# Moving the transposes of an attention and gated-layer kernel from TensorE to the DMA crossbar

## The chip, the cores and the metric

The kernel runs on one core of one Trainium2 chip. The metric is the time of one execution in microseconds of device time. Each run states how many executions it had, and gives their median with the lowest and highest. Every experiment ran beside the kernel before on the same chip.

## The reference, cut to what matters

Four batches of block-sparse attention (8 heads, 768 rows, head size 64; a window of 16 around each row, plus one maximum of k and one mean of v for each block of 32 rows) feed a gated layer of 512 inputs and 1536 hidden values. All inputs and the output are 32-bit floats in DRAM.

```python
k_sum = k.reshape(B, H, nb, 32, D).max(axis=3)
v_sum = v.reshape(B, H, nb, 32, D).mean(axis=3)
scores_l = where(|i - j| < 16, scale * q @ k.T, -1e9)
scores_s = scale * q @ k_sum.T + log(32)
a = softmax(concat([scores_l, scores_s]))
attn = a @ concat([v, v_sum])
x = attn.transpose(0, 2, 1, 3).reshape(B * S, H * D)      # 3072 x 512
out = (sigmoid(x @ w_gate) * (x @ w_val)) @ w_out
```

The kernel's matmuls sum along the partitions of their tiles. So q and k are turned, to have the head size on the partitions, and so are the normalised values, to have the 512 channels on them. These three transposes are what the change moves.

## The kernel before

While TensorE works on batch b's layers, the attention of batch b+1 is slipped in between as small units. A unit is a letter and a pair of heads: T transposes q and k of pair p and makes the block maxima, S makes scores and their exponentials, V the means of v, A multiplies with v and normalises, X transposes the result into xT, the input of the layers. The order of the units fixes the order of every engine's instructions.

```python
def load_qk(tap, b, p, half=None, queue=None):          # whole rows, uncast, SyncE
    (queue or nc.sync).dma_start(out=st..., in_=tap[b, 2*p:2*p+2, ...])

def T(self, p, h=None):
    self.transposed(pk, self.src[p][0])     # 6 x nc.tensor.transpose into PSUM
    self.transposed(pq, self.src[p][1])     # 6 more
    self.natural(kTn[:, 16:16 + S], pk)     # ScalarE copy out of PSUM
    self.natural(self.qT[p]..., pq)         # ScalarE copy out of PSUM
    nc.vector.tensor_reduce(...max...)      # then two VectorE copies into kTx
    ...
def X(self, p, h=None):
    ...                                     # 6 x nc.tensor.transpose of xs
    nc.scalar.copy(out=self.xT[:, p, o:o + n], in_=br[:, 0:n])

def replicate(self, t0):                    # spreads the means: vx <- vx, SyncE
    nc.sync.dma_start(out=vx[96:120, t0:NQ]..., in_=vx[96:120, 0:1]...to_broadcast(...))

def load_next(b):                           # q, k: load, then cast on GpSimd
    for p in range(NP):
        s_ = (load_qk(k, b, p), load_qk(q, b, p))
        srcs[b][p] = [cast_qk(s_[0], "pool"), cast_qk(s_[1], "pool")]

REST  = "Q0 Q1 S0b Q2 S1b Q3 S2b S3b A0b A1b X0b A2b X1b A3b X2b X3b"   # batch 0, half 2
FIRST = "T0 T1 S0a S0b T2 S1a S1b T3 S2a S2b V S3a S3b"                 # batch 1
LAST  = "- - A0 A1 X0 A2 X1 A3 X2 X3"
NEXT  = "- - T0 T1 S0a S0b T2 S1a S1b T3 S2a S2b S3a S3b - - A0 A1 X0 A2 X1 A3 X2 X3"
# [...] the layers of a batch, with the units spread among them
spread(m1[0] + m1[1] + ffn.units2(), extra, 0, 33)
```

v and all weights already come by casting loads from GpSimd (32-bit in DRAM, 16-bit in the on-chip memory). v's rows are 64 values of one head, so its pieces are 128 bytes as written.

The softmax here doesn't subtract the row's maximum and nothing guards it: scores larger than these inputs give would overflow.

Of the kernel before, what the change touches and what calls it, by code (L numbers as in the profile page):

```python
# [8 lines left out]
FP32 = mybir.dt.float32  # L9
BF16 = mybir.dt.bfloat16  # L10
# [6 lines left out]
def kernel(  # L17
# [10 lines left out]
    nc = tc.nc  # L28

    B, H, S, D = q.shape  # L30
# [4 lines left out]
    NS = S // 32  # L35
    KX = W + NS
    NP = H // 2
# [3 lines left out]
    HALF = S // 2  # L41

    const = ctx.enter_context(tc.tile_pool(name="const", bufs=1))
    stg_pool = ctx.enter_context(tc.tile_pool(name="stg", bufs=8))
    bf_pool = ctx.enter_context(tc.tile_pool(name="bf", bufs=10))
    vm_pool = ctx.enter_context(tc.tile_pool(name="vmp", bufs=2))
    qT_pool = ctx.enter_context(tc.tile_pool(name="qTp", bufs=4))
    p_pool = ctx.enter_context(tc.tile_pool(name="pp", bufs=4))
    xs_pool = ctx.enter_context(tc.tile_pool(name="xsp", bufs=2))
    xT_pool = ctx.enter_context(tc.tile_pool(name="xTp", bufs=2))  # L50
    hT_pool = ctx.enter_context(tc.tile_pool(name="hTp", bufs=2))
    gate_pool = ctx.enter_context(tc.tile_pool(name="gatep", bufs=3))
# [9 lines left out]
    def view(ap, off, dims):  # L62
        return bass.AP(ap.tensor, ap.offset + off, [list(ap.ap[0])] + [list(d) for d in dims])
# [5 lines left out]
    kTn_t = [const.tile([128, S + 32], BF16, name=f"kTn{i}") for i in range(2)]  # L69
# [51 lines left out]
        else:  # L121
            nc.gpsimd.tensor_copy(out=out, in_=in_)  # L122

    def load_qk(tap, b, p, half=None, queue=None):

        n = S if half is None else HALF
        s0 = 0 if half is None else HALF * half
        T = n // 128
        st = stg_pool.tile([128, 2, 6, 64], FP32, name="qkst", tag="stg")
        (queue or nc.sync).dma_start(  # L130
            out=st[:, :, 0:T, :].rearrange("p h t d -> p h (t d)"),
            in_=tap[b, 2 * p:2 * p + 2, s0:s0 + n, :].rearrange("h (p t) d -> p h (t d)", t=T),
        )
        return st[:, :, 0:T, :]

    def cast_qk(st, eng):
        T = st.shape[2]
        bf = bf_pool.tile([128, 6, 2, 64], BF16, name="qkbf", tag="qkbf")[:, 0:T]
        copy(eng, bf, st.rearrange("p h t d -> p t h d"))
        return bf  # L140

    def load_v(b, t0, t1):

# [23 lines left out]
    class Attention:  # L167
        def __init__(self, b, src, xT):


            self.b, self.src, self.xT = b, src, xT
            self.vx = vx_t[b % 2]
            self.kTx, self.qT, self.P, self.xs = {}, {}, {}, {}
            self.vm, self.ms = {}, {}

        def transposed(self, dst, src):
# [4 lines left out]
        def natural(self, dst, src):  # L181
# [2 lines left out]
            nc.scalar.copy(out=dst.rearrange("p (a t) -> p a t", t=T),  # L184
                           in_=src[:, 0:128 * T].rearrange("p (t a) -> p a t", t=T))

        def T(self, p, h=None):

            at = psum2.tile([128, 2, 1024], BF16, name="tp", tag="at")
            pk, pq = at[:, 0], at[:, 1]  # L190
            self.transposed(pk, self.src[p][0])
            self.transposed(pq, self.src[p][1])
            kTn, kTx = kTn_t[kT_ctr[0] % 2], kTx_t[kT_ctr[0] % 4]
            kT_ctr[0] += 1
            self.kTx[p] = kTx
            self.qT[p] = qT_pool.tile([128, S], BF16, name="qT", tag="qT")
            self.natural(kTn[:, 16:16 + S], pk)
            self.natural(self.qT[p][:, 0:S if h is None else HALF], pq)
            nc.vector.tensor_reduce(  # L199
                out=kTx[:, 0, W:KX],  # L200
                in_=kTn[:, 16:16 + S].rearrange("p (n w) -> p n w", w=32),
                axis=AX.X, op=ALU.max)
            nc.vector.tensor_copy(out=kTx[:, :, 0:W], in_=view(kTn, 0, [[QT, NQ], [1, W]]))  # L203
            nc.vector.tensor_copy(
                out=kTx[:, 1:NQ, W:KX],
                in_=kTx[:, 0:1, W:KX].to_broadcast([128, NQ - 1, NS]))

        def Q(self, p, h=None):

            pq = psum2.tile([128, 2, 1024], BF16, name="tp", tag="at")[:, 1]  # L210
            self.transposed(pq, self.src[p][2])
            self.natural(self.qT[p][:, HALF:S], pq)

        def S(self, p, hf):
            kTx, qT = self.kTx[p], self.qT[p]
# [42 lines left out]


        def L(self, g, h=None):  # L260
            st = self.vm[g] = vm_pool.tile([4 * NS, 32, 64], FP32, name="vm", tag="vm")
            nc.sync.dma_start(
                out=st.rearrange("p w d -> p (w d)"),
                in_=v[self.b, 4 * g:4 * g + 4].rearrange("h (n w) d -> (h n) (w d)", w=32))
            self.ms[g] = vm_pool.tile([4 * NS, 64], FP32, name="ms", tag="ms")
# [24 lines left out]
        def A(self, p, h=None):  # L290
# [6 lines left out]
            for t in range(6 * g0, 6 * g1):  # L297
# [14 lines left out]
                in1=rec[:, 0:G].to_broadcast([128, G, 6, 64]),  # L312
                op=ALU.mult)
            self.xs[p] = xs

        def X(self, p, h=None):
            n = S if h is None else HALF
# [62 lines left out]
    def spread(base, extra, lo, hi):  # L380

        n, m, j = len(base), len(extra), 0
        for i, u in enumerate(base):
            u()
            if i >= lo:
                want = min(m, (m * (i + 1 - lo) + (hi - lo) - 1) // (hi - lo))
                while j < want:
                    extra[j]()
                    j += 1
        while j < m:  # L390
            extra[j]()
            j += 1
# [6 lines left out]

    a0 = att[0]  # L400

    sk = [load_qk(k, 0, p) for p in range(NP)]
    sq = [load_qk(q, 0, p, half=0, queue=nc.scalar) for p in range(NP)]

    def cast0(p):
        srcs[0][p] = [cast_qk(sk[p], "dve"), cast_qk(sq[p], "act")]
# [28 lines left out]


    def load_next(b):
        for p in range(NP):
            s_ = (load_qk(k, b, p), load_qk(q, b, p))
            srcs[b][p] = [cast_qk(s_[0], "pool"), cast_qk(s_[1], "pool")]  # L440

    for p in range(NP):
        srcs[0][p].append(cast_qk(load_qk(q, 0, p, half=1), "pool"))
    for i in range(6):
        load_wo(i)
    load_next(1)
    load_v(1, 0, NQ)

    REST = "Q0 Q1 S0b Q2 S1b Q3 S2b S3b A0b A1b X0b A2b X1b A3b X2b X3b"
    FIRST = "T0 T1 S0a S0b T2 S1a S1b T3 S2a S2b V S3a S3b"  # L450
    LAST = "- - A0 A1 X0 A2 X1 A3 X2 X3"
    MEANS = "R0a R0b R0c R0d M0 R1a R1b R1c R1d M1 - B".split()
    NEXT = "- - T0 T1 S0a S0b T2 S1a S1b T3 S2a S2b S3a S3b - - A0 A1 X0 A2 X1 A3 X2 X3".split()

    def loads(b):
        if b < B:
# [5 lines left out]
    for b in range(B):  # L462
        ffn = f0 if b == 0 else Ffn(b, xTs[b])
        m1 = [[(lambda f=f, hf=hf: ffn.m1(f, hf)) for f in range(NF)] for hf in range(2)]
        if b == 0:
            spread(m1[0][1:], a0.units(REST), 2, 10)
            extra = att[1].units(FIRST) + [lambda: loads(2)] + att[1].units(LAST)
            spread(m1[1] + ffn.units2(), extra, 4, 23)
        else:
            extra = []  # L470
            if b + 1 < B:
                both = [x for pair in zip(MEANS, NEXT) for x in pair]
                extra = (att[b + 1].units(" ".join(both)) + [lambda: loads(b + 2)]
                         + att[b + 1].units(" ".join(NEXT[len(MEANS):])))
            spread(m1[0] + m1[1] + ffn.units2(), extra, 0, 33)


# [28 lines left out]
```

## Time and profile before

| | before |
|---|---|
| time, median of 3 (lowest to highest) | 261.75 us (260.33 to 263.04) |
| span of the profiled execution | 259.5 us |
| TensorE busy | 241.0 us |
| holes in TensorE after 28 us (sum of its timeline's idle times) | 2.3 us |
| first layer matmul of batch 0, 1, 2, 3 | 26.7, 95.2, 152.4, 208.7 us |

The last row is the ruler in this kernel. It cuts the span at the starts of the four batches.

The page cuts the span in 40 slices of 6.5 us. A digit is the busy share of a slice in tenths, PEclk the granted clock of TensorE, DMA the mean busy share of the 16 DMA engines:

```profile
PE   1567899999999998999999999999999999999993
...
PEclk9999999999999999999999999999999999999999
DMA  6999999999308999900199999000211220000132
```

TensorE is full from the sixth slice on and its clock is whole. From the twelfth slice on the DMA row has gaps: the transfers come in bursts with rest between.

### The profile page before, as it was taken

What the parts mean: (1) busy time and instruction counts of PE and PEld (TensorE: products, weight loads), DVE (VectorE), ACT (ScalarE), POOL (GpSimd) and SP (SyncE); (2) the same over time, 40 slices, a digit from 0 to 9 for tenths busy, and PEclk for the clock granted to TensorE, in tenths of its full rate; (3) what the DMA queues carried; (4) which work ended last, traced back from release to release, by engine and by line L of the source; (5) the groups of instructions that cost most, each with busy time, mean ns of one, the idle gap of its engine ahead of it and who ended that gap; (6) DMA issues with size and microseconds to landing.
All of it is one profiled execution on the core that took longest, in us unless ns stands there. A gap on an engine that the chain in (4) does not pass through costs nothing.

```text
span 259.5 us, 5305 instructions
## 1 busy us (share of the span) xinstructions
PE 241.0 (93%) x2136; PEld 137.7 (53%) x2136; DVE 133.8 (52%) x263; ACT 124.5 (48%) x217; POOL 77.1 (30%) x111
## 2 busy tenths in 40 slices
PE   1567899999999998999999999999999999999993
PEld 1432455666644555666555556666555556666441
DVE  5865237648733318888645227988543124444000
ACT  2850347538942434766742435766533433333111
POOL 8998059377000279400002893000000000000000
PEclk9999999999999999999999999999999999999999
DMA  6999999999308999900199999000211220000132
GB/s 223 230 165 170 222 269 278 269 121 123 18 16 230 314 401 134 101 4 1 26 234 317 360 132 133 1 3 1 46 40 51 75 82 0 0 3 1 40 121 81
DMA packets 60912, 32.70 MB, mean 126 GB/s; under 512 B 40624, under 2 KB 57432, under 8 KB 60504
## 3 DMA queue, kind: packets, MB, share of 16 engines
q0 software_dynamic: 45632, 9.31, 41.4%
q1 hardware_dynamic: 14168, 22.28, 27.3%
q10 hardware_dynamic: 1088, 0.79, 0.9%
q8 instruction: 16, 0.26, 0.4%
q14 instruction: 8, 0.07, 0.1%
HBM read 34.34 MB, written 6.29 MB: 157 GB/s over the span
## 4 chain that ended last, share of the span: by engine, by line
PE 82%; DMA 9%; ACT 3%; DVE 2%; issue 1%; SPq 0%; ACTq 0%
PE gp L350 25%; PE vp L350 24%; PE m L367 19%; PE tp L178 4%; DMA qkst<-in_k_dram 3%; DMA out_dram<-ot 3%; PE sc L223 3%; PE vsp L240 3%; DMA qkst<-in_q_dram 3%; PE av L300 2%; PE br L321 2%; ACT kTn L184 1%; DVE kTx L199 1%; DVE vx L120 1%; ACT ot L372 1%
## 5 line engine op out<-in xcount | busy, mean ns | idle before, releaser
L358 DVE SCALAR_TENSOR_TENSOR hT<-gate,vp 128x384 bf16<-128x384 f32 x96 | 52.4, 548 | 56.1 <-PE vp L350 45.2
L350 PE MATMUL gp<-xT,wg 128*128 128x384 bf16 x384 | 80.2, 330 | 1.1 <-ACT xT L324 1.1
L350 PE MATMUL vp<-xT,wv 128*128 128x384 bf16 x384 | 79.6, 329 | 0.8 <-ACT ot L372 0.8
L367 PE MATMUL m<-wo,hT 128*128 128x512 bf16 x288 | 67.1, 380 | 0.0
L357 ACT ACTIVATE gate<-gp 128x384 f32<-128x384 f32 x96 | 47.4, 495 | 40.8 <-DVE hT L358 29.2
L350 PEld LDWEIGHTS <-wv 128*128 128x128 bf16 x384 | 37.8, 98 | 27.3 <-issue 3.0
L350 PEld LDWEIGHTS <-wg 128*128 128x128 bf16 x384 | 35.5, 99 | 21.7 <-issue 0.5
L122 POOL CAST qkbf<-qkst 128x768 bf16<-128x768 f32 (+1 forms) x28 | 22.5, 813 | 78.3 <-DMA qkst<-in_k_dram 38.6
L367 PEld LDWEIGHTS <-hT 128*128 128x128 bf16 x288 | 26.3, 98 | 28.4 <-issue 0.4
L372 ACT ACTIVATE ot<-m 128x512 f32<-128x512 f32 x24 | 14.3, 597 | 47.4 <-PE m L367 44.8
L147 POOL DMA_DIRECT2D vx<-in_v_dram x48 | 36.5, 774 | 0.6 <-DMA vx<-in_v_dram 0.4
L229 ACT ACTIVATE P<-sc 128x768 bf16<-128x768 f32 x32 | 26.0, 815 | 10.9 <-PE sc L223 10.8
L230 DVE TENSOR_TENSOR P<-P,mask 128x768 bf16<-128x768 bf16 x32 | 18.7, 585 | 13.3 <-ACT P L229 13.1
L178 PE MATMUL tp<-ident,qkbf 128*128 128x128 bf16 x192 | 15.5, 236 | 7.7 <-DVE qkbf L120 5.9
L199 DVE TENSOR_REDUCE kTx<-kTn 128x24 bf16<-128x768 bf16 x16 | 15.2, 951 | 7.8 <-ACT kTn L184 7.8
L178 PEld LDWEIGHTS <-qkbf 128*128 128x128 bf16 x192 | 13.4, 106 | 9.8 <-DVE qkbf L120 7.0
L324 ACT COPY xT<-br 128x768 bf16<-128x768 bf16 (+1 forms) x20 | 13.3, 669 | 10.9 <-PE br L321 10.9
L184 ACT COPY kTn<-tp 128x768 bf16<-128x768 bf16 x16 | 12.8, 799 | 9.3 <-PE tp L178 8.7
L268 DVE TENSOR_REDUCE ms<-vm 96x16 f32<-96x512 f32 x16 | 16.4, 1023 | 0.0
L309 DVE TENSOR_TENSOR xs<-av,rec 128x768 bf16<-128x768 f32 (+1 forms) x20 | 15.9, 797 | 0.7
L307 DVE RECIPROCAL rec<-av 128x12 f32<-128x12 f32 (+1 forms) x20 | 4.3, 216 | 22.3 <-PE av L300 22.3
L223 PE MATMUL sc<-qT,kTx 64*128 64x64 bf16 x384 | 12.1, 197 | 3.1 <-DVE kTx L203 2.9
(46 smaller groups left out, 112.0 us busy)
## 6 DMA issues: line engine op xcount, KB each, us to landing
qkst<-in_k_dram SPq DMA_DIRECT2D x16, 384.0 KB
out_dram<-ot SPq DMA_DIRECT2D x24, 256.0 KB
qkst<-in_q_dram SPq DMA_DIRECT2D x12, 384.0 KB
vx<-in_v_dram POOLq DMA_DIRECT2D x40, 96.0 KB, 4.7
vm<-in_v_dram SPq DMA_DIRECT2D x4, 768.0 KB
wo<-in_moe_w_out_dram POOLq DMA_DIRECT2D x6, 256.0 KB, 13.6
wg<-in_moe_w_gate_dram POOLq DMA_DIRECT2D x5, 256.0 KB, 8.0
wv<-in_moe_w_val_dram POOLq DMA_DIRECT2D x5, 256.0 KB, 9.8
```

The source lines that it names most:

```text
L122: nc.gpsimd.tensor_copy(out=out, in_=in_)
L147: nc.gpsimd.dma_start(out=vx_t[b % 2][r0:r0 + hi - lo, t, :, 0:64], in_=v[b, :, lo:hi, :].transpose([1, 0, 2]))
L178: nc.tensor.transpose(dst[:, 128 * t:128 * (t + 1)], src[:, t].rearrange("p h d -> p (h d)"), ident)
L199: nc.vector.tensor_reduce(out=kTx[:, 0, W:KX], in_=kTn[:, 16:16 + S].rearrange("p (n w) -> p n w", w=32), axis=AX.X, op=ALU.max)
L223: nc.tensor.matmul(out=sc[:, i, QT * t6:QT * (t6 + 1)], lhsT=kTx[64 * i:64 * i + 64, t, :], rhs=qT[64 * i:64 * i + 64, QT * t:QT * (t + 1) ...
L229: nc.scalar.activation(out=Ph, in_=sc[:, :, 0:6 * QT], func=ACT.Exp, scale=SCALE)
L230: nc.vector.tensor_tensor(out=Ph, in0=Ph, in1=mask[:, None, 6 * hf:6 * hf + 6, :].rearrange("p i t w -> p i (t w)") .to_broadcast([128, 2, ...
L350: nc.tensor.matmul(out=o, lhsT=wb[:, c, 128 * f:128 * (f + 1)], rhs=self.xT[:, c, HALF * hf:HALF * (hf + 1)], start=(c == 0), stop=(c == N ...
L357: nc.scalar.activation(out=gate, in_=gp, func=ACT.Tanh, scale=0.5)
L358: nc.vector.scalar_tensor_tensor(out=self.hT[hf][:, f, :], in0=gate, scalar=1.0, in1=vp, op0=ALU.add, op1=ALU.mult)
L367: nc.tensor.matmul(out=self.m3, lhsT=self.hT[hf][:, f, 128 * tt:128 * (tt + 1)], rhs=wo_bf[:, f], start=(f == 0), stop=(f == NF - 1))
L372: nc.scalar.mul(out=ot, in_=self.m3, mul=0.5)
```

## The change

The intent: TensorE is the bound, and a transpose is no arithmetic. So q and k of batches 1 to 3, half of q of batch 0, and nearly all normalised values are transposed by DMAs from the on-chip memory to itself through the crossbar, issued by SyncE. That also saves the ScalarE copies out of PSUM. The crossbar DMAs here read 16-bit tiles, so q and k now come by casting loads from GpSimd, one per head, in 128-byte pieces. D issues the two crossbar DMAs of a pair, K makes the maxima from them, E does half of q of batch 0, Y replaces X.

```diff
+    def load_nat(tap, b):
+        nat = nat_pool.tile([128, NP, 6, 128], BF16, name="nat", tag="nat")
+        for h in range(H):
+            nc.gpsimd.dma_start(
+                out=nat[:, h // 2, :, 64 * (h % 2):64 * (h % 2) + 64],
+                in_=tap[b, h].rearrange("(c p) d -> p c d", p=128))
+    def load_half(tap, b): ...       # three such loads for the second half of q, batch 0
 [...]
+        def D(self, p, h=None):
+            self.begin(p)
+            for dst, nat in ((self.kTn[p][:, 16:16 + S], self.src[0]), (self.qT[p], self.src[1])):
+                nc.sync.dma_start_transpose(
+                    out=dst.rearrange("p (c t) -> p c t", c=6),
+                    in_=nat[:, p].rearrange("p c d -> p (c d)"))
+        def E(self, c, h=None):
+            nc.sync.dma_start_transpose(out=qT0[:, :, HALF + 128 * c:HALF + 128 * (c + 1)], in_=...)
+        def Y(self, p, h=None):
+            nc.sync.dma_start_transpose(out=self.xT[:, p, 128 * c0:128 * c1]..., in_=self.xs[p]...)
 [...]
     def load_next(b):
-        for p in range(NP):
-            s_ = (load_qk(k, b, p), load_qk(q, b, p))
-            srcs[b][p] = [cast_qk(s_[0], "pool"), cast_qk(s_[1], "pool")]
-    for p in range(NP):
-        srcs[0][p].append(cast_qk(load_qk(q, 0, p, half=1), "pool"))
+        srcs[b][0], srcs[b][1] = load_nat(k, b), load_nat(q, b)
+    srcs[0]["q1"] = load_half(q, 0)
+    load_next(1)                     # now ahead of the output weights
     for i in range(6):
         load_wo(i)
-    load_next(1)
     load_v(1, 0, NQ)
-    REST = "Q0 Q1 S0b Q2 S1b Q3 S2b S3b A0b A1b X0b A2b X1b A3b X2b X3b"
-    FIRST = "T0 T1 S0a S0b T2 S1a S1b T3 S2a S2b V S3a S3b"
-    LAST = "- - A0 A1 X0 A2 X1 A3 X2 X3"
-    NEXT = "- - T0 T1 S0a S0b T2 S1a S1b T3 S2a S2b S3a S3b - - A0 A1 X0 A2 X1 A3 X2 X3".split()
+    REST = "E0 E1 E2 - S0b S1b S2b A0b Y0b S3b A1b Y1b A2b Y2b A3b Y3b"
+    FIRST = "D0 D1 - - K0 D2 S0a S0b K1 D3 S1a S1b K2 S2a S2b K3 S3a S3b V"
+    LAST = "- A0 Y0 A1 Y1 A2 Y2 A3 Y3"
+    NEXT = "- D0 D1 - - K0 D2 S0a S0b K1 D3 S1a S1b K2 S2a S2b K3 S3a S3b - A0 Y0 A1 Y1 A2 Y2 A3 Y3".split()
 [...]                               # limits of the three spreads 1 to 3 lower
```

V has moved in FIRST, from before S3a to the very end. Not shown are smaller staging pools, which make room; experiment 3 keeps them and costs next to nothing.

## The prediction

> **What bounds the kernel now.** I read the page first, then the table of stretches, the chain of waits, and TensorE's timeline. The page's first part:
>
> ```profile
> PE 241.0 (93%) x2136; PEld 137.7 (53%) x2136; DVE 133.8 (52%) x263; ACT 124.5 (48%) x217; POOL 77.1 (30%) x111
> ```
>
> TensorE leads and nothing else is near it. But 93% is an average, so I cut the span at the stages (columns: stretch, length, busy time of PE, PEld, DVE, ACT, POOL, clock, DMA share, GB/s):
>
> ```profile
> 0.00:32.00 32.00, 18.55 (x165) 10.79 (x166) 18.55 (x51) 13.36 (x25) 23.43 (x42) 1.00 1.48 201
> 32.00:52.00 20.00, 20.00 (x214) 12.14 (x213) 12.14 (x24) 11.88 (x24) 12.46 (x17) 1.00 1.19 272
> ...
> 75.00:98.00 23.00, 22.27 (x229) 11.38 (x229) 5.88 (x10) 8.75 (x14) 7.00 (x9) 1.00 0.86 274
> 98.00:133.00 35.00, 34.95 (x324) 21.44 (x323) 28.47 (x53) 22.43 (x40) 8.70 (x12) 1.00 0.67 70
> ...
> 189.40:208.80 19.40, 19.40 (x196) 9.98 (x194) 5.73 (x10) 6.66 (x10) 0.00 (x0) 1.00 0.19 69
> ```
>
> After a start of 32 us (whose holes are 13.45 us) TensorE has no hole but 0.73 us in 75 to 98 and small change. Time taken off TensorE after 32 us should come off the end one for one, if what replaces it arrives in time. So the question is what a transpose really occupies on TensorE. The groups, shapes kept apart:
>
> ```profile
> L178 PE MATMUL tp<-ident,qkbf 128*128 128x128 bf16 x192 | 15.5, 236 | 7.7 <-DVE qkbf L120 5.9 <-ACT qT L184 1.9
> L321 PE MATMUL br<-ident,xs 128*128 128x128 bf16 x96 | 9.2, 231 | 1.0 <-DVE xs L309 1.0
> ```
>
> The 236 ns is the latency of one; they overlap. The chain gives the cost in line (start, us, what):
>
> ```profile
> 102.11 0.65 PE vp L350 x4
> 102.76 0.67 PE tp L178 x12
> 103.43 0.65 PE gp L350 x4
> ```
>
> Twelve transposes take 0.67 us between two matmul groups that are not slowed: 56 ns each. The timeline shows the same of the other kind (start, us; six begin at 204.48 and the next matmul at 204.81, so 0.33 us, 55 ns each):
>
> ```profile
> 204.48 0.50 PE L321 MATMUL br<-ident,xs 128*128 128x128 bf16 x6
> 204.81 4.05 PE L367 MATMUL m<-wo,hT 128*128 128x512 bf16 x18
> ```
>
> **What the Trainium skill says.**
> (1) "VectorE: DVE Perf Modes", section "The three transpose paths", gives 390 ns for a 128x128 bf16 transpose on TensorE and 1309 ns by the DMA crossbar. This trace disagrees on the first as a cost (56 ns in a row); the second is not in it.
> (2) "DMA: Bandwidth & Descriptors", section "Latency and other measured facts", gives DMA transposes 261 GB/s with a non-contiguous middle dimension, some 350 to 400 when contiguous. No run yet shows this; it contradicts (1) by an order if the 1309 ns were serial (32 KB in 1309 ns is 25 GB/s).
> (3) The same page, "Issuing engines are not separate DMA queues": DMAs from all queues run on the same 16 engines and interleave. The trace agrees: in the stretches where GpSimd's and SyncE's transfers run together the share sums above 1 (1.19 in 32 to 52).
> (4) "TensorE: Matmul & The Clock Gate", section "Why this matters for your kernels": an idle gap over some 3 us makes TensorE fall back to its slower state. The trace has something like it: after the start with holes, the first group of four matmuls takes 1.28 us (at 32.11), later ones 0.65.
>
> **The change, part by part.**
>
> *Off TensorE.* Of the 192 q/k transposes, batch 0 keeps 24 for k and 12 for the first half of q; 156 go. Of the 96 value transposes the 12 of batch 0's first half stay; 84 go. 240 x 0.056 = 13.4 us, all of it after 32 us, on the path.
>
> *Off ScalarE.* The copies from PSUM: 12 kTn x 0.80 + 12 qT x 0.81 + 4 x 0.48 + 12 xT x 0.80 + 4 x 0.48 = 32.8 us of 124.5. ScalarE isn't the bound (22.4 of 35 us in the attention stretch): nothing directly.
>
> *Off GpSimd, and the loads.* 24 casts at 0.86 us and 4 at 0.51 go. In their place GpSimd issues casting loads: 16 per batch for three batches and 3 for half of q, 51 in all at about 0.77 us as for v's, 39 us. GpSimd rises to about 94 us, not the bound. SyncE's queue no longer carries q and k. That undoes one wait: the chain holds 80.27 to 88.8 in k loads, then an output store until 97.30, on which ScalarE's ot copy and then TensorE waited. Its hole of 0.78 us goes.
>
> *Crossbar transfers added on SyncE.* 24 for q and k, 12 whole and 4 half ones for the values, 3 for batch 0's half q: 43, some 7.9 MB. For one middle batch, from rows of this trace: q/k loads 16 x 0.77 = 12 us, v 12 x 0.76 = 9 us, v means and outputs 3.1 MB at the 273 GB/s of 80 to 85 us = 11.5 us, crossbar 12 x 0.197 MB at the skill's 261 GB/s = 9 us (estimate). 42 us against a period of about 52: it fits, so DMA doesn't become the bound on average. What counts is the latency where TensorE's order is fixed. Three places:
>
> (a) *Batch 0, second half of q.* It now queues behind the weights on GpSimd's ring. v of batch 0 and the gate and value weights are 1.15 + 3.15 = 4.3 MB as written; by the table in steps of 5 us, 2.58 MB of that had moved at 25 us (all traffic from 10 to 25 us at 154, 162 and 174 GB/s, and 0.12 earlier). The other 1.72 MB at 174 to 185 GB/s end near 34.5. Then 0.39 MB of q at the 130 GB/s seen for v's rows (60 to 65 us) end near 37.5. Landing, issue and transfer of the last of three crossbar DMAs I estimate at 3 to 4 us (an ordinary first k load takes 3.8 us from issue to its cast here): 41. TensorE comes to the scores of that half after four weight columns, the last ending at 36.6 as in the old timeline. A wait of some 4 us (2 to 7) that was not there, and 1 us for a TensorE gone cold.
>
> (b) *Batch 1 in batch 0's layers.* k and q of batch 1 land about 42 and 48, v near 66: in time. But D2 and D3 wait for a kTn buffer, which K0 and K1 on VectorE free, and K3 and S3a stand in the same slot: with 3.5 us per pair of crossbar DMAs, K3's 1.7 us (0.95 + 0.47 + 0.26) can come late by 1.5 us.
>
> (c) *Three batch borders.* After the last A3, five units of 1.3 us remain, and the fourth chunk of xT is needed 0.5 us into the next batch: 7.0 us. Needed: normalisation 0.2 + 1.0, an output store that stands ahead of Y3 on SyncE and waits for its matmuls and copy (ready 2.1 us after A3, issue 0.4), crossbar 3.5 to 4: 6 to 6.5 us, with v and q loads on the same engines. I put 0.6 us on each, 1.8 us in all. In the middle of a batch D0 has about 12 us before its scores: no wait.
>
> Sum: 261.75 - 13.4 - 0.8 + 5 + 1.5 + 1.8 = 255.85. Whoever chose the new spacing (lower spread limits, empty slots after D and E) seems to have laid it out to cover the latencies, so I shade the waits by 1 us: 255.
>
> **Rivals.**
> *Everything hidden*: TensorE stays gapless, 247.5. For: 9 to 15 us of slack for D in the unit order, no other engine near its limit. Against: (a), which follows from bytes and rates already in the trace.
> *The crossbar is slow* (nearer the 1309 ns a block): 72 blocks per batch would be 94 us, more than the period. Even at three times my cost, D2 and D3 run late, K stalls VectorE in order and with it hT, and every border waits 4 to 8 us: 270 to 300. For: two figures of the skill disagree. Against: 16 engines share the blocks.
> *The casting loads crowd the ring*: small 128-byte pieces lengthen the start and the borders, with Y behind 1.5 MB of v rows on SyncE's ring; 259 to 264. For: shares over 2 whenever v streams. Against: v's stream already keeps up with GpSimd's issue (12 in 9.1 us) under busy TensorE.
>
> **Range and chances.** All hidden gives 247.5, my waits doubled about 264, so 247.5 to 263 holds 8 in 10. The 2% line is 256.5, close above my sum, and the laid-out spacing speaks for the good side: faster 0.62, same 0.26, slower 0.12.
>
> **What would show it.** tp falls to 36 and br to 12 transposes, TensorE's busy sum to about 227; L122's 28 casts on GpSimd are gone; output stores no longer wait behind k loads. For (a): a hole in TensorE of 2 to 7 us between 36 and 42, ended by a qT from a DMA, matmuls slow just after it. For (b): a wait of sc for kTx near 70. For (c): a hole at the first gp of each batch, ended by xT from a DMA. A period between batches of about 51 to 52.5 us (before 54.5 and 56.3). I am wrong if the crossbar DMAs take over 5 us each in the middle batches, or if no hole appears at (a).

## The result, and the profile after

| | before | after |
|---|---|---|
| time, median of 4 (lowest to highest) | 261.56 us (260.33 to 263.04) | 289.63 us (287.81 to 291.18) |
| profiled span | 259.5 us | 287.3 us |
| TensorE busy | 241.0 us | 236.2 us |
| holes in TensorE after 28 us | 2.3 us | 34.8 us |
| first layer matmul of batch 0, 1, 2, 3 | 26.7, 95.2, 152.4, 208.7 us | 25.6, 122.6, 182.4, 236.5 us |

The change made the kernel slower: the ratio is 1.1068, with a 95% interval of 1.0978 to 1.1158. A ratio here is the mean time of one kernel's fast runs over that of the other's of the same rounds, so it is not quite the ratio of the quoted medians.

The same rows of the page, and its busy line:

```profile
PE 236.2 (82%) x1882; PEld 127.6 (44%) x1896; DVE 132.7 (46%) x263; ACT 96.4 (34%) x173; POOL 96.5 (34%) x134
...
PE   2676605976995949949999799999998999999994
...
PEclk9997965995999896989999999999999999999999
DMA  7999999999999999999923937533060550000022
```

TensorE has lost its full rows between the sixth and the eighteenth slice (7.2 us each), its clock drops in the same slices, and the DMA engines are full from the second slice to the twentieth without one gap. After that all three rows look like before's. The kernel is lost in its first half and healthy in its second.

The transposes went as planned. The group of before with 192 q and k transposes, and that of 96 values, are now:

```profile
L201 PE MATMUL tp<-ident,qkbf 128*128 128x128 bf16 x36 | 4.5, 308 | 6.5 <-DVE qkbf L121 5.7 <-ACT nat L207 0.8
...
L367 PE MATMUL br<-ident,xs 128*128 128x128 bf16 x12 | 1.8, 283 | 1.2 <-DVE xs L348 1.2
```

36 and 12 are the counts predicted. What took their place is in the table of TensorE's waits (engine, what waits, what it waited for; us in total, times, longest):

```profile
PE sc L262 <- DMA nat<-nat: 11.8, 3, 8.3
PE sc L262 <- DVE kTx L248: 10.3, 9, 2.3
PE gp L396 <- DMA xT<-xs: 8.9, 5, 2.8
...
PE av L339 <- DMA vx<-vx: 4.1, 1, 4.1
```

The first is E (half of q of batch 0), the second K (the maxima), the third Y, the fourth the DMA that spreads the means of v. The K row also holds 3 us of the start; the rest sums to 32 us, nearly the whole list of new holes. E, Y and the spread, 24.8 us together, wait for a DMA from the on-chip memory to itself. K doesn't, although K reads what D delivers: VectorE sat idle before none of the four reductions of batch 1. The chain of waits before the longest of these holes has no DMA in it (start, us, what):

```profile
88.28 0.34 PE sc L262 x10
...
89.35 0.81 ACT P L268
...
90.67 0.55 DVE hT L404
91.21 0.86 DVE kTx L244
92.07 0.38 DVE kTx L248
...
92.50 0.59 PE sc L262 x12
```

Scores of one pair, their exponentials, VectorE's queue with K in it, and the scores of the next pair follow each other, because the order puts K directly before the scores that need it. (q of this pair landed at 91.5 us, so an earlier K alone would have won 1 us of this hole.)

TensorE's timeline at the first of them (start, length; in brackets the idle time before and what ended it):

```profile
33.32 0.81 PE L396 MATMUL vp<-xT,wv 128*128 128x384 bf16 x4
42.46 0.29 PE L262 MATMUL sc<-nat,kTx 64*128 64x64 bf16 x4 [8.33 <-DMA nat<-nat]
44.52 0.29 PE L262 MATMUL sc<-nat,kTx 64*128 64x64 bf16 x4 [1.77 <-DMA nat<-nat]
46.49 0.61 PE L262 MATMUL sc<-nat,kTx 64*128 64x64 bf16 x16 [1.68 <-DMA nat<-nat]
47.03 1.46 PE L396 MATMUL gp<-xT,wg 128*128 128x384 bf16 x4
...
52.81 0.82 PE L396 MATMUL gp<-xT,wg 128*128 128x384 bf16 x4
```

One hole of 8.3 us and two small ones; and four matmuls then take 1.46 us that take 0.82 later. The chain of waits tells how the 8.3 us come about (start, us, what):

```profile
25.68 10.70 DMA nat<-in_q_dram
36.40 1.29 SPq L226
37.79 1.27 SPq L226
39.15 7.29 DMA nat<-nat
46.49 0.61 PE sc L262 x16
```

q's load stands behind the weights until 36.40. Then each of the three crossbar DMAs takes 1.3 us to issue, and the last one lands 7.3 us after its issue began. Three more DMAs of the on-chip memory to itself stand in the chain in this way: a Y of batch 0 at 59.11 (8.73 us), the spread of the means at 100.93 (6.25 us) and a Y of batch 1 at 118.63 (8.74 us). In the second half of the same execution, with no loads of q, k and v left, the same crossbar DMA lands in 2.5 to 2.6 us where nothing runs beside it (those issued at 142.17 and 143.61, for instance), and in 4.1 us at most.

The table of stretches shows what runs meanwhile (stretch, length, busy time of PE, PEld, DVE, ACT, POOL, clock, DMA share, GB/s):

```profile
40.00:45.00 5.00, 0.58 (x8) 0.30 (x8) 0.00 (x0) 0.00 (x0) 4.94 (x7) 0.50 2.29 157
45.00:50.00 5.00, 3.51 (x36) 1.79 (x35) 1.23 (x3) 2.00 (x3) 4.17 (x6) 0.50 2.36 157
```

GpSimd is the busiest engine: it issues casting loads. They keep the DMA engines more than full (2.3, since a share counts each piece from its start to its end, and pieces overlap) at 157 GB/s. The clock of TensorE is halved.

The whole difference, from the two profiled spans:

| part | us |
|---|---|
| 240 transposes gone, at the 56 ns of the prediction | -13.4 |
| holes at E: 8.33 + 1.77 + 1.68 | 11.8 |
| holes at Y of batch 0: 0.59 + 2.40 + 1.89 | 4.9 |
| holes at K of batch 1, ended by VectorE: 0.65 + 0.38 + 1.01 + 0.20 + 2.32 | 4.6 |
| hole at the spread of batch 1's means | 4.05 |
| holes at the border to batch 1: 1.27 + 2.78 | 4.05 |
| holes at K of batches 2 and 3: 0.65 + 1.02, twice | 3.3 |
| other holes after 28 us, less the 2.3 that before had | -0.1 |
| left over, for the most part matmuls at half clock | 8.6 |
| sum (287.3 - 259.5) | 27.8 |

The left-over row agrees with a count of its own: in stretches of 5 us from 28 us on, the sum of TensorE's busy time times the missing share of the clock is 10.5 us; before has some of that too in its start. By the ruler, 27.4 us of the 27.8 are lost before batch 1's layers begin. From there to batch 2 it is 59.8 us against 57.2, from batch 2 to 3 it is 54.1 against 56.3, and the end is equal.

### The profile page after: what moved, and what is told of

Read it like the earlier page. It is cut to its first block, busy times and chain, and to the rows that moved or that the text cites. A ratio compares the mean times of both kernels' runs of the same rounds, so it can differ in the third digit from the quotient of the medians.

```text
span 287.3 us, 4851 instructions
## 1 busy us (share of the span) xinstructions
PE 236.2 (82%) x1882; PEld 127.6 (44%) x1896; DVE 132.7 (46%) x263; ACT 96.4 (34%) x173; POOL 96.5 (34%) x134
## 4 chain that ended last, share of the span: by engine, by line
PE 64%; DMA 20%; DVE 5%; issue 3%; POOL 3%; ACT 3%; SPq 1%; DVEq 0%; POOLq 0%; ACTq 0%
PE m L413 20%; PE gp L396 19%; PE vp L396 18%; DMA xT<-xs 6%; DMA nat<-in_q_dram 4%; DMA vx<-in_v_dram 3%; PE sc L262 3%; PE av L339 3%; DMA nat<-nat 3%; DMA vx<-vx 2%; DMA wv<-in_moe_w_val_dram 2%; DVE kTx L244 2%; ACT P L268 2%; DVE hT L404 2%; PE vsp L279 1%
## 5 line engine op out<-in xcount | busy, mean ns | idle before, releaser
L396 PE MATMUL gp<-xT,wg 128*128 128x384 bf16 x384 | 82.9, 337 | 10.1 <-DMA xT<-xs 8.9
L396 PE MATMUL vp<-xT,wv 128*128 128x384 bf16 x384 | 81.7, 335 | 0.0
L396 PEld LDWEIGHTS <-wg 128*128 128x128 bf16 x384 | 36.8, 100 | 29.7 <-issue 7.3
L413 PEld LDWEIGHTS <-hT 128*128 128x128 bf16 x288 | 27.2, 100 | 32.7 <-issue 3.7
L262 PEld LDWEIGHTS <-kTx 64*128 64x128 bf16 x384 | 9.0, 101 | 34.1 <-issue 17.8
L151 POOL DMA_DIRECT2D nat<-in_q_dram x24 | 19.7, 863 | 8.5 <-DMA nat<-in_k_dram 7.7
L151 POOL DMA_DIRECT2D nat<-in_k_dram x24 | 19.7, 833 | 7.9 <-DMA vx<-in_v_dram 5.2
L262 PE MATMUL sc<-nat,kTx 64*128 64x64 bf16 x96 | 4.7, 230 | 15.2 <-DMA nat<-nat 11.8
L262 PE MATMUL sc<-qT,kTx 64*128 64x64 bf16 x288 | 9.0, 195 | 8.0 <-DVE kTx L248 7.3
L339 PE MATMUL av<-vx,P 120*64 120x65 bf16 x384 | 11.3, 208 | 4.7 <-DMA vx<-vx 4.1
```

The costliest lines, as they stand in the source:

```text
L151: nc.gpsimd.dma_start(out=nat[:, h // 2, :, 64 * (h % 2):64 * (h % 2) + 64], in_=tap[b, h].rearrange("(c p) d -> p c d", p=128))
L262: nc.tensor.matmul(out=sc[:, i, QT * t6:QT * (t6 + 1)], lhsT=kTx[64 * i:64 * i + 64, t, :], rhs=qT[64 * i:64 * i + 64, QT * t:QT * (t + 1) ...
L339: nc.tensor.matmul(out=av[r:r + 64, t // 6, (t % 6) // 2, i, 0:65], lhsT=P[0:KX, i, t, :], rhs=vx[0:KX, t, 2 * p + i, 0:65], start=True, s ...
L396: nc.tensor.matmul(out=o, lhsT=wb[:, c, 128 * f:128 * (f + 1)], rhs=self.xT[:, c, HALF * hf:HALF * (hf + 1)], start=(c == 0), stop=(c == N ...
L413: nc.tensor.matmul(out=self.m3, lhsT=self.hT[hf][:, f, 128 * tt:128 * (tt + 1)], rhs=wo_bf[:, f], start=(f == 0), stop=(f == NF - 1))
```

## The experiments

The question was which property made the new waits so long. My theories: (1) the casting loads of q and k, in 128-byte pieces, crowd the DMA engines; (2) the crossbar DMA is slow beside any load; (3) the order of the units leaves too little room; (4) the clock.

**1. no_qk_loads**: all 48 casting loads of q and k replaced by a fill. The inputs are wrong, though the result passed the comparison: with inputs of 0.1 the scores hardly matter.

```diff
-        for h in range(H):
-            nc.gpsimd.dma_start(out=nat[:, h // 2, :, ...], in_=tap[b, h]...)
+        nc.gpsimd.memset(nat, 0.01)
```

> The changed kernel with the 48 casting loads of q and k of batches 1 to 3 taken away: GpSimd fills those tiles with a constant instead, so the result is wrong on purpose; all 43 crossbar transfers and v's and the weights' casting loads stay. Crowding theory (crossbar transfers are slow only while 128-byte casting pieces run on the same DMA engines): the first crossbar transfers, which then have no casting stream behind them but the output weights, land about 2.5 us after issue instead of 6.0 to 7.3; the hole before the second half's scores falls from 11.8 us to some 7.5 (their issue still waits for q behind the weights), most of the others go, total 262 to 272. Rival, crossbar transfers that follow each other on SyncE are slow by themselves: landing stays at 6 us and over in batches 0 to 2, total above 280.

Measured: 286.0 us (3 runs), ratio 1.0954 (1.0846 to 1.1061). My theory (1) fell at once. The hole at E became longer, not shorter:

```profile
43.83 0.29 PE L259 MATMUL sc<-nat,kTx 64*128 64x64 bf16 x4 [9.77 <-DMA nat<-nat]
```

What ran beside E now were the output weights, which had moved up, in 1024-byte pieces. E's three DMAs landed in 6.8, 8.8 and 10.1 us.

**2. pe_on_casting**: the change's casting loads, but all transposes back on TensorE, with before's order of units. This is the other half of the change alone.

```diff
-            for dst, nat in (...): nc.sync.dma_start_transpose(...)
+            for i, (dst, nat) in enumerate(...):
+                for c in range(6):
+                    nc.tensor.transpose(at[:, i, 128 * c:128 * (c + 1)], nat[:, p, c], ident)
+                nc.scalar.copy(out=dst, in_=at[:, i, 0:S])
```

> The changed kernel's casting loads kept, but every transpose back on TensorE with copies from PSUM (no crossbar transfer at all). Crowding theory: TensorE only waits about 2 us for batch 0's second half of q; 261 to 266. Rival, the casting loads deliver q and k too late whatever transposes them: holes before the transposes of batches 1 and 2 of several us, over 275.

Measured: 277.0 us (3 runs), ratio 1.0582 (1.0496 to 1.0669), but the experiment had a fault of mine. In the table of waits:

```profile
PE tp L223 <- ACT kTn L224: 11.0, 12, 1.3
```

I had put k's copy between the transposes of k and of q, which share a PSUM tile, so TensorE waited for ScalarE 12 times. It says nothing of the loads until mended.

**3. pe_on_casting2**: the same with both copies after all 12 transposes.

```diff
-                nc.scalar.copy(out=dst, in_=at[:, i, 0:S])
+            nc.scalar.copy(out=self.kTn[p][:, 16:16 + S], in_=at[:, 0, 0:S])
+            nc.scalar.copy(out=self.qT[p], in_=at[:, 1, 0:S])
```

> pe_on_casting had a fault of mine: q's six transposes were issued behind k's copy from the same PSUM tile, and TensorE waited 0.89 us for it 12 times. Here both are transposed before the copies, as in the kernel before. Casting loads kept, no crossbar transfer. If the casting loads by themselves cost little: 262 to 267 (the wait for the second half of q, 2 us, stays). If they are late by themselves: over 270, with waits of TensorE for nat.

Measured: 262.12 us (3 runs), ratio 1.008 (0.9999 to 1.0162): the same as before. The casting loads fill the DMA engines here too (until the 18th slice of 6.5 us), and by the interval that costs 1.6% at most: all that TensorE waits for a DMA is 1.2 us for q's load. The loads by themselves explain 4 of the 28 us at most.

**4. wide_both**: the opposite half. Loads stay as before's (uncast, in large pieces), and q, k and the values of batches 1 to 3 go through the crossbar. Batches 2 and 3 are loaded from GpSimd's queue.

```diff
+        def D(self, p, h=None):
+            for i in range(2):
+                tn = tn_pool.tile([128, 6, 128], BF16, name="tn", tag="tn")
+                nc.sync.dma_start_transpose(out=tn, in_=self.src[p][i]...)
+        def K(self, p, h=None):        # ScalarE copies tn into natural order, then the maxima
+        def Y(self, p, h=None):        # as in the change
+        qu = None if b == 1 else nc.gpsimd
-    FIRST, LAST, NEXT of before
+    FIRST, LAST, NEXT of the change
```

> The kernel before with q, k of batches 1 to 3 and their normalised values transposed by the crossbar, but q and k loaded as before without cast in pieces of 1.5 KB (for batches 2 and 3 from GpSimd's queue), cast on GpSimd, and put into natural order by ScalarE after the crossbar; batch 0 stays on TensorE. Crowding theory: crossbar transfers land in 2.5 to 4 us, the 12.1 us of transposes of batches 1 to 3 come off, small waits stay: 247 to 255. Rival, the crossbar is slow beside any loading traffic: landing at 6 us and over while 1.5 KB pieces run, waits at K and at the batch borders, 262 or more.

Measured: 299.36 us (4 runs), ratio 1.1414 (1.1301 to 1.1527), the slowest of all; I had expected a gain. Batch 1's crossbar DMAs stood behind its own loads on SyncE's queue and landed after 8.5 to 18.6 us; the last pair of it, beside v's rows and then the 4608-byte pieces of the next batch's loads, after 12 and 17 us, which made a hole of 10.88 us at K. The spread of the means, an ordinary DMA of 264 pieces of 1056 bytes with no crossbar in it, fared no better:

```profile
111.49 0.71 PE L330 MATMUL av<-vx,P 120*64 120x65 bf16 x19 [11.23 <-DMA vx<-vx]
```

So it needs neither casting, nor 128-byte loads, nor the crossbar: a short DMA was slow beside every kind of load that these runs have. The piece records of the traces show how the two share: count how many pieces of each kind begin per microsecond while both queues have work.

| run, time | companion pieces | crossbar pieces (256 bytes) per us | companion pieces per us |
|---|---|---|---|
| changed kernel, around 143.5 us | none | 1120 (560 in half a us) | - |
| no_loads_reordered (run 10), 35 to 38 us | 512 bytes (weights) | 245, 254, 248 | 244, 251, 246 |
| no_qk_loads, 44 to 47 us | 1024 bytes (output weights) | 154, 164, 165 | 152, 169, 164 |
| wide_both, 77 to 83 us | 4608 bytes, one in six 1536 (k, q rows) | 104, 104, 105, 108, 111, 105 | 102, 101, 107, 109, 110, 103 |

The counts are equal, as if the two queues took turns piece by piece, whatever the pieces hold (the counts include the few 4-byte pieces that signal completion; the records don't name the DMA engine, so single turns can't be seen). The kernel before shows the same between its loads, GpSimd's in 512 bytes and SyncE's in 768 and 1536, so it could have been read before the change: from 32 to 40 us, in stretches of 2 us, 386 and 390 pieces of the two queues, 334 and 333, 293 and 295, 294 and 293. A crossbar DMA of this kernel is 768 pieces (512 for E, 384 for a Y of batch 0). By the table, as an estimate, 768 pieces take 3.1 us at 245 per us, 4.7 us at 165, and 7.3 us at 105, to which issue and start come; alone it lands in 2.5 us in all.

Two things don't fit this simple picture. The start is late too: the first piece of E in the changed kernel began 2.9 us after its issue, that of the first Y 3.9 us after, against 1.2 us alone. And beside the 128-byte pieces of the changed kernel the counts are not equal: from 40 to 45 us 349, 92, 365, 382 and 326 crossbar pieces per us against 397, 928, 554, 794 and 678.

**5. wide_values**: as wide_both, but only the values go through the crossbar.

```diff
 # on wide_both
-    FIRST = "D0 D1 - - K0 D2 S0a S0b K1 D3 S1a S1b K2 S2a S2b K3 S3a S3b V"
-    NEXT  = "- D0 D1 - - K0 D2 S0a S0b ... S3a S3b - A0 Y0 A1 Y1 A2 Y2 A3 Y3"
+    FIRST of before
+    NEXT  = "- - T0 T1 S0a S0b T2 ... S3a S3b - A0 Y0 A1 Y1 A2 Y2 A3 Y3"
```

> As wide_both, but the crossbar for the normalised values of batches 1 to 3 alone; q and k on TensorE. 72 transposes of 56 ns are 4.0 us, 0.8 us of the old wait for a store behind loads may go too: crowding theory 256 to 260, with Y landing in 2.5 to 4 us. Rival (slow crossbar): a wait for xT of 3 us and more at each of three borders, 265 or more.

Measured: 274.28 us (268.07 to 279.77, 4 runs). Three of the four were slow, and the one fast run, 268.07, is above the expected range too. The profiled execution, itself a slow one, has holes of 1.14, 1.76, 3.23 and 6.89 us before the first matmuls of batch 1, all ended by Y, whose DMAs landed 11 to 13 us after issue beside the loads of batch 2. All four executions are above the 263.67 us that before reached at most in that session, which suggests that Y alone, at one border, is enough to lose; it isn't shown.

**6. batch0_pe**: the change with the second half of batch 0 as before (loads from SyncE, cast on GpSimd, transposed by TensorE).

```diff
-    srcs[0]["q1"] = load_half(q, 0)
+    for p in range(NP):
+        srcs[0][p].append(cast_qk(load_qk(q, 0, p, ..., half=1), "pool"))
-    REST = "E0 E1 E2 - S0b S1b ... A3b Y3b"
+    REST = "Q0 Q1 S0b Q2 S1b Q3 S2b S3b A0b A1b X0b A2b X1b A3b X2b X3b"
```

> The changed kernel with one part undone: batch 0's second half (q and the normalised values) back on TensorE with q loaded uncast on SyncE as before; batches 1 to 3 unchanged. The theory now (a crossbar transfer alone lands in 2.5 us, but beside any load it takes turns with it and takes 5 to 10, and each wait also lets TensorE's clock fall): the holes of 11.8 and 4.9 us and their cold stretches go, 266 to 272; K, replicate and border waits of batch 1 stay. Rival (the loss is mainly in batch 1's waits for K and means, which slide with it): above 277.

Measured: 275.17 us (3 runs), ratio 1.0504 (1.0376 to 1.0631). About half of the loss goes with the holes at E and at batch 0's Y. Of the rest, this run's trace (a slow execution) still has 4.16 us before the last scores of batch 1, here ended by q's crossbar DMA itself, 5.18 at the means and 1.73 + 3.12 at the border. Batch 0's place in the kernel is only the worst of several.

**7. no_loads**: the change without GpSimd's loads of q, k and v for batches 1 to 3 (SyncE still loads v's rows for the means), and with the output weights after E. Wrong (relative error 1.41).

```diff
+        nc.gpsimd.memset(nat, 0.01)                        # for q and k
-    load_v(1, 0, NQ)
+    nc.gpsimd.memset(vx_t[1][:, :, :, 0:64], 0.01)         # for v
+    def wo_after():                                        # after E2
+        nc.gpsimd.tensor_copy(out=mark, in_=qT0[:, 3, S - 1:S])
+        for i in range(6): load_wo(i)
```

> All 43 crossbar transfers with next to nothing beside them: q, k and v of batches 1 to 3 are not loaded (tiles filled by GpSimd, wrong result on purpose), and the output weights are loaded only when batch 0's last crossbar transfer of q has landed. Turn-taking theory: crossbar transfers land in 2.5 to 3.5 us throughout, the hole before the second half's scores is some 7 us (q still comes behind the weights), no holes at Y and at the borders, the ones at K of 1.7 us a batch stay: 254 to 264. Rival (crossbar chains are slow in batches 0 and 1 for another reason): landing stays above 5 us there, over 272.

Measured: 272.27 us (3 runs), ratio 1.0446 (1.0369 to 1.0522). Some 17 us of the 28 are gone, and E's crossbar DMAs land in 2.5, 2.4 and 2.5 us. But I had expected 254 to 264 and landings of 2.5 to 3.5 us throughout; the time is in the range that I had given to the rival, and the Ys of batch 0, beside the output weights, still took 4.1 to 7.9 us. And holes stay even where the transfer is quick:

```profile
39.53 0.29 PE L259 MATMUL sc<-nat,kTx 64*128 64x64 bf16 x4 [5.18 <-DMA nat<-nat]
```

At E, q's load behind the weights is the cause (issue at 36.97, as late as in the change). At the means the same trace has a hole of 2.47 us, and the cause is V, which the change moved to the end of FIRST: the spread now has nothing to hide behind (run 8 moves V back, and the hole is gone). The order of the program has a share of its own. So has the instrument: at the third pair of batch 1 two copies of VectorE take 2.05 and 2.75 us beside GpSimd's fills, instead of 0.45 and 0.23 (see run 10), and TensorE has holes of 2.62 and 2.47 us there. The loads are thus worth more than these 17 us.

**8. after_reordered**: the change with nothing but its order altered. q of batch 0 is loaded before the last three pairs of weights, each K comes one unit of scores earlier, and V before K3.

```diff
     for f0, nf in (...):
+        if f0 == 6:
+            srcs[0]["q1"] = load_half(q, 0)
-    FIRST = "D0 D1 - - K0 D2 S0a S0b K1 D3 S1a S1b K2 S2a S2b K3 S3a S3b V"
+    FIRST = "D0 D1 - - K0 D2 S0a K1 D3 S0b S1a K2 S1b S2a V K3 S2b S3a S3b"
-    NEXT  = "- D0 D1 - - K0 D2 S0a S0b K1 D3 S1a S1b K2 S2a S2b K3 S3a S3b - ..."
+    NEXT  = "- D0 D1 - - K0 D2 S0a K1 D3 S0b S1a K2 S1b S2a K3 S2b S3a S3b - ..."
```

> The changed kernel with its order alone mended, no work taken away: q's casting load of batch 0's second half ahead of the last three pairs of gate and value weights, each K one score unit ahead of its scores, V ahead of K3 so that the spread of the means is done before A0. If order is a large part of the loss: the first crossbar transfers are issued about 30 instead of 36.4, their hole falls from 11.8 to under 4 us, the waits for K and for the spread of the means from 8.6 to some 3 together, 268 to 275. If contention is nearly all of it: over 280.

Measured: 271.48 us (3 runs, one slow), ratio 1.0359 (1.029 to 1.0429), inside the expected range. Order alone wins 18 us back. The spread has no hole any more, and of the waits for K after the start only 0.65 us is left. The other holes left are E (0.43 + 2.02), Y of batch 0 (3.41 + 1.97) and the border (1.34 + 3.49 + 2.24): the places where a Y or an E has no more room, and still lands beside loads.

**9. late**: a version meant to win. Batches 0 and 1 stay as before, so no crossbar DMA runs in the crowded first third. Batches 2 and 3 use casting loads and the crossbar, with K early.

```diff
     def load_next(b):
+        if b > 1:
+            srcs[b][0], srcs[b][1] = load_nat(k, b), load_nat(q, b)
+            return
-    NEXT = "- - T0 T1 S0a S0b T2 ... X2 X3"
+    NEXT = "- D0 D1 - - K0 D2 S0a K1 D3 S0b S1a K2 S1b S2a K3 S2b S3a S3b - A0 Y0 A1 Y1 A2 Y2 A3 Y3"
     # [...] smaller staging buffers, to make room for nat
```

> A version meant to beat both: batches 0 and 1 as in the kernel before (TensorE), batches 2 and 3 with casting loads and crossbar for q, k and values, where little else is loading, and each K placed one score unit ahead of its scores. Turn-taking theory: 8.1 us of transposes go, few waits come: 250 to 257. Rival: border and K waits eat it, 260 or more.

Measured: 259.55 us (257.43 to 262.22, 4 runs, one slow), ratio 0.9938 (0.983 to 1.0045): the same as before. D, which has about 12 us of room, waits nowhere for long. Two things eat the gain in the profiled execution, itself the slow one: V waits 1.84 us for v of batch 1, whose loads now come late on GpSimd, and the border to batch 2 has 1.78 + 2.44 us, Y beside batch 3's loads, with a slow clock after it.

**10. no_loads_reordered**: runs 7 and 8 together. Its output is wrong, which doesn't matter for the time.

```diff
 # on no_loads
+        if f0 == 6:
+            srcs[0]["q1"] = load_half(q, 0)
-    FIRST, NEXT of the change
+    FIRST, NEXT of after_reordered
```

> no_loads with the same mended order: crossbar transfers with next to no loads beside them and each wait given room (wrong result on purpose). If contention and order together are the whole loss, this is near the 247.5 us that I had called everything hidden: 246 to 255. If a third cause remains: over 258.

Measured: 262.85 us (258.65 to 263.99, 3 runs, two slow), above the expected 246 to 255 even in its fast run; by the expectation's own line (over 258) a third cause remains. The borders are as hoped: no hole there, and 52.3 us from batch to batch. A third cause can be named, but it is one of the instrument: the fills that stand for the loads hold up VectorE, and TensorE behind it. In the timelines of VectorE and GpSimd:

```profile
73.94 2.30 DVE L245 COPY kTx<-kTn 128x1152 bf16<-128x1152 bf16 x1
```

```profile
73.27 5.57 POOL L150 MEMSET nat<- 128x3072 bf16 x2 [22.25 <-DMA kTn<-nat]
```

The copy takes 0.45 us elsewhere. The Trainium skill, "SBUF — State Buffer", section "SBUF: two separate sides", says that VectorE in some of its modes and GpSimd share one pair of ports under an exclusive lock: the later one blocks until the other's whole instruction is done. This trace agrees, with 2.30 us against 0.45. In its other places E still waited 3.36 us, because its crossbar DMAs, now early, ran beside the weights and landed in 6.9 to 9.1 us. The run thus can't say what the change is worth without any load beside it.

**11. warm**: the change with 44 filler matmuls in the hole at E, to keep TensorE's clock up.

```diff
+    def fill():
+        z = ps([128, 512], FP32, "fill")
+        for _ in range(44):
+            nc.tensor.matmul(out=z, lhsT=ident, rhs=wg_bf[:, 0, 0:512], start=True, stop=True)
-    REST: E0 E1 E2 -    S0b ...
+    REST: E0 E1 E2 fill S0b ...
```

> The changed kernel with 44 matmuls of 512 columns (9.4 us at full clock, of no use, into a PSUM tile of their own) put where TensorE waits for the second half of q, so that it does not stand idle there. If the granted clock falls because TensorE stood idle: full clock from 45 to 55 us instead of 0.5 and 0.83, and 1.5 to 3.5 us less, 286 to 288.5. If the clock falls for another reason: the same 0.5 and 0.83 and no gain, 289 to 292.

Measured: 289.67 us (285.46 to 291.18, 5 runs, two slow), ratio 1.0993 (1.0914 to 1.1071). The stretches after the hole:

```profile
45.00:50.00 5.00, 4.38 (x71) 2.65 (x71) 2.95 (x7) 3.41 (x6) 4.55 (x7) 1.00 2.25 164
50.00:55.00 5.00, 5.00 (x61) 2.82 (x60) 3.63 (x9) 1.98 (x4) 4.22 (x6) 1.00 1.23 202
```

The clock is whole where it was 0.50 and 0.83. So the half clock at this hole follows from idleness, and isn't a second effect of the DMA traffic. In time the gain isn't resolved: the median stands in the range of the other expectation, the intervals of this run and of the changed kernel overlap, and the profiled execution lost part of it again at the means, where the hole grew from 4.05 to 5.7 us.

**12. late2**: late with its two faults mended. v of batch 1 is loaded between the casts of batch 1, and the values of batch 2 are transposed by TensorE, so that no Y stands beside loads.

```diff
     for p in range(NP):
+        if p > 1:
+            load_v(b, 6 * p - 12, 6 * p - 6)
-    load_v(1, 0, NQ)
+    def nexts(b):
+        return NEXT[:-8] + "A0 A1 X0 A2 X1 A3 X2 X3".split() if b == 2 else NEXT
```

> late with its remaining holes mended: v of batch 1 is issued between the casts of q and k (TensorE waited 1.8 us for it), and batch 2's normalised values go back to TensorE, since their crossbar transfers met the loads of batch 3 (holes of 1.8 and 2.4 us and slow clock after them). q, k of batches 2 and 3 and values of batch 3 by crossbar. Turn-taking theory: 252 to 257. Rival (no version with crossbar transfers beats before by 2%): 258 or more.

Measured: 253.03 us (252.48 to 255.32, 8 runs), ratio 0.9669 (0.9629 to 0.9709): 3.3% faster than before, and correct. It is the best version. All that TensorE waits for after 100 us is in three lines of its timeline, the first of which is a crossbar DMA:

```profile
129.29 0.35 PE L263 MATMUL sc<-qT,kTx 64*128 64x64 bf16 x12 [0.62 <-DMA qT<-nat]
...
134.16 0.57 PE L340 MATMUL av<-vx,P 120*64 120x65 bf16 x22 [1.26 <-DMA vx<-vx]
```

(The third is 0.16 us between two output matmuls.) Batch 2's crossbar DMAs are no quicker here: those issued from 96 to 121 us land in 6.8 to 10.7 us. They have the room for it. By count, 120 transposes are gone from TensorE (96 of q and k, 24 of batch 3's values), 6.7 us at 56 ns; the remaining 2 us of the gain I did not separate.

## Why the prediction was wrong

The size of the removed work was right and the waits were not. The prediction's sum was "261.75 - 13.4 - 0.8 + 5 + 1.5 + 1.8 = 255.85". By terms:

- **Removed transposes, 13.4 us.** Right in count (36 and 12 left). Their worth shows where nothing waits: batch 2 to batch 3 takes 54.1 us against 56.3, although two waits for K of 1.7 us together are in it. The busy sum came out at 236.2 instead of 227, because matmuls at half clock are longer.
- **ScalarE, GpSimd and the store behind k's loads.** Right in the main: GpSimd 96.5 us (predicted 94), ScalarE 96.4 us (the prediction's terms give 91.7), and the 0.78 us before 98 us is gone. None of it was the bound.
- **(a) E, 4 us and 1 us of cold clock.** The mechanism was right, and q was there a little sooner than reckoned (issue at 36.40, against near 37.5). The term that was mis-sized most is that of the three crossbar DMAs, "Landing, issue and transfer", put at 3 to 4 us: from 36.40 to 46.45 it took 10 us. The second is TensorE's arrival, taken as 36.6 from the old timeline: it stood there from 34.1 us. The wait was 11.8 us, and the clock stayed at half from 38.0 to 51.7 us.
- **(b) K of batch 1, 1.5 us.** It was 4.6 us, and the path was another. D did land late (in 8 to 10 us, then 5 to 7, where the prediction reckoned with 3.5 per pair), but no K waited for it: K stood in VectorE's order directly before its scores, as the chain above shows. With D at 2.5 us, batches 2 and 3 have 1.67 us each in the same places, for which the prediction gave nothing. The wait for the spread of the means, 4.05 us, was not foreseen at all: the prediction gives the new place of V no cost. That DMA isn't a crossbar DMA, yet in wide_both it leaves the longest hole of all.
- **(c) Borders, 0.6 us each.** It was 4.05 at the border to batch 1 and none at the other two. The prediction treated the three as alike, but no loads are left at the last two: GpSimd runs ahead and has issued the last one by 136 us. One part of the wait lies in SyncE's own queue: v's rows for the next means, 192 pieces of 8192 bytes issued from 101.83 us on, begin between 103.9 and 114.2 us, and the first Y, issued at 109.33, begins behind them at 114.6. The third rival had named this ("Y behind 1.5 MB of v rows on SyncE's ring"); no run separates it from the loads of GpSimd.
- **Clock, 1 us in all.** About 9 us. It is a consequence of the holes, as warm shows.

The step that failed under (a), (c) and the spread is "42 us against a period of about 52: it fits, so DMA doesn't become the bound on average", with landings of 3.5 to 4 us beside it. The sentence is true and was the wrong question. The average tells whether the engines keep up over a period. It doesn't tell how long a short transfer takes while another queue has work: in the first 140 us that was 5 to 11 us, with a later start and a shared piece rate, instead of 2.5. GpSimd's queue never ran dry from the start to 140 us (the DMA row of the page), so every short DMA of the first half had a companion. The prediction did say what would make it wrong, "if the crossbar DMAs take over 5 us each in the middle batches", and it is this sign that came: 5.3 to 10.4 us in batch 1.

The prediction also took a DMA share above 1 as a sign that two queues interleave. It isn't one: from 46 to 49 us of the changed kernel GpSimd's queue alone has pieces, and the share is 2.40.

Of the rivals, "the casting loads crowd the ring" named the right place at the border to batch 1 and was too small by 25 us; and its blame on small pieces fell with no_qk_loads and wide_both. "The crossbar is slow" got the size (270 to 300), but not by its reason: alone the DMA lands in 2.5 us, so its six blocks take 0.42 us each in all, far below the 1.3 us a block that this rival rested on.

What is shown, then: the slow landing beside loads of four piece sizes; its absence without loads; that order alone makes up 18 of the 28 us and loads alone at least 17 (they overlap, since a hole is the landing time less the room that the order gives, and either closes it); and a version that keeps the slow landings but gives them room, and wins. What stays open: why beside 128-byte pieces the turns are not as even as in the table above, and why the first piece comes late. There are also stretches, as from 64 to 65 us in the changed kernel, in which 298 pieces of the two queues begin, against some 1200 at 46 us, and at 66.3 us single pieces take 1.1 to 1.2 us. I did not find what they wait for. Nor do I know how much of the 9 us a warm clock alone would give back in time.

## What to carry to other kernels

Before work is moved from an engine to a DMA, look up for each new DMA which other queue has work at that moment, and reckon its landing as a late start plus its number of pieces times the time of one turn, not as bytes over bandwidth; here 2.5 us became 5 to 11. (This is an estimate, and beside 128-byte pieces a rough one.) Then give it that much room in the order of the program, or put it where no loads run. Look in the same way at the steps that stay on an engine: K waited for its place in the order and not for its DMA. A version that moved only the transposes with room to spare won 3.3%, where moving all of them lost 10.7%.

## What the Trainium skill lacked or had wrong

- "DMA: Bandwidth & Descriptors", section "Issuing engines are not separate DMA queues", says that DMAs of all queues interleave. The grain is in its section "Queues, rings and completion order", which the prediction passed over: each DMA engine goes round the queues that have work and takes a whole packet, typically 9 to 17 descriptors, from each. The equal counts here (245 and 244 per us beside 512 bytes, 154 and 152 beside 1024, 104 and 102 beside 4608) agree with such rounds; whether a turn is a piece or a packet they don't tell, and beside 128-byte pieces they were not equal. What the page lacks is what follows for time: a DMA of 256-byte pieces that lands alone in 2.5 us took 5 to 19 us beside loads.
- The same page, section "Rules for kernel authors", says that a transpose next to ordinary DMAs needs nothing. That holds for correct results here. For time it needs room: the holes that waited for a transpose came to 20.7 us.
- "VectorE: DVE Perf Modes", section "The three transpose paths": a block on TensorE, given as 390 ns, costs 56 ns in a row here. 1309 ns for the crossbar is too high for larger DMAs: six blocks land in 2.5 us from issue, and SyncE issues one such DMA in 1.21 to 1.29 us.
- I found on no page, for this chip, that SyncE's issue bounds short crossbar DMAs: 0.197 MB each 1.25 us is 157 GB/s at best, while a burst alone moves 560 pieces of 256 bytes in half a microsecond, 287 GB/s.
- "TensorE: Matmul & The Clock Gate", section "Why this matters for your kernels", warns of gaps over some 3 us. The trace agrees for the longer holes (half clock from 38.0 to 51.7 us after the hole at E), but a hole of 2.32 us, from 90.2 to 92.5 us, was enough too (half clock from 92.7 to 96.1 us). In all it cost about 9 us.
